# Moving the first layer-1 key tile one tile forward at each change of layer, with longer FFN steps and other banks for their products

## The chip, the cores and the metric

The kernel runs on one core of one Trainium2 chip. The metric is the device time of one execution in microseconds (us), quoted as the median of several executions. Engines are called as the profile calls them: PE is TensorE's matmuls, PEld its weight loads, DVE is VectorE, ACT is ScalarE, POOL is GpSimd, SP issues the loads.

## The reference, cut to what matters

Two identical layers of single-token decoding run one after the other, with the same weights and the same key and value cache:

```python
# B = 8 batches, one new token each, D = 640, 32 heads of Dh = 128, Sk = 4096 cached keys, Dff = 1728, bf16
x = x + attention(layernorm(x), k_cache, v_cache, wq, wo)   # layer 0
x = x + relu_ffn(layernorm(x), w1, w2)
x = x + attention(layernorm(x), k_cache, v_cache, wq, wo)   # layer 1, the same cache again
x = x + relu_ffn(layernorm(x), w1, w2)
```

Each layer reads the whole cache. Layer 1 of a batch can't begin before that batch has been through the FFN of layer 0, because its queries are made from the result.

## The kernel before

The work is cut into *visits*: one visit is one pair of heads of one batch in one layer, so 16 x 8 x 2 = 256 visits. A visit has a key tile (K) and a value tile (V). Each tile consists of four *units* of 512 KB; a unit lives in one of 26 slots of an *arena* in on-chip memory. When PE has read the last of a unit, its slot is free and the next load into it can be issued. Up to 21 slots keep tiles of layer 0 for layer 1 of the same batch, so that they need not be loaded twice.

The place that matters here is the *turn*: layer 0 of a batch ends, its FFN has to run, and then layer 1 of the batch begins. There are eight turns, one per batch. To cover the FFN, the kernel puts two layer-0 visits of the *next* batch in between ("ahead"). Call these tiles K0, V0, K1, V1, and call the first key tile of layer 1 L. L is one of the kept tiles: it needs no load, and running it sets four slots free. The order of tiles is made here, and the line with `turns` is the one in question:

```python
    slots = []
    for i in range(NV + 1):
        pair = [("K", i)] * (i < NV) + [("V", i - 1)] * (i >= 1)
        ends = i and visits[i - 1][0] == 0 and last_of[visits[i - 1][:2]] == i - 1
        turns = 0 < i < NV and visits[i][0] == 1 and visits[i - 1][0] == 0
        slots += pair[::-1] if ends or turns else pair      # before, at a turn: K0 K1 V0 V1 L
```

(The last turn differs: no next batch is left, so the two visits in between are layer-1 visits of the batch before, `turns` does not hold, and the order was K0 K1 V0 L V1 already.)

The FFN of layer 0, the norm behind it and the first two layer-1 queries form one *chain* of steps. A step is a handful of matmuls with one column each; it is put into the gap behind a unit's matmuls, so that PE always has the next unit soon. `CAP` limits how many matmuls go into one gap. The number in `own` is the matmuls of a step:

```python
CAP = 20
...
        for k in range(n_up):                        # n_up = 5: 3 of 14 row groups each
            c += [own(15, "up", k)]
            ...
        c += [own(0, "relu")] + [own(14, "down", k) for k in range(n_down)] + [own(0, "add")]   # n_down = 5
        c += [own(2, "mean"), own(0, "center")] + query(b, 0)
        c += [own(1, "var2"), own(0, "root2")] + query(b, 1)
...
        if which == "K":
            if layer:
                until(("QC", b, hp))                 # the query of this visit has to be there
```

Results of matmuls lie in three banks of the result memory (PSUM): `o_ps` (output of the V tiles), `s_ps` (scores) and `small_ps` (everything small, the FFN's products too):

```python
            h = [ffn_ps[:, :FC].rearrange("p (f b) -> p f b", b=1)] * len(up_parts)   # ffn_ps is part of small_ps
            y = ffn_ps[:, FC * B : FC * B + DC].rearrange("p (c b) -> p c b", b=1)
```

## Time and profile before

| what | value | read from |
|---|---|---|
| time | 2341.08 us, median of 3 (2338.69 to 2342.32) | the times |
| read from device memory | 988.08 MB | the page, DMA queues |
| rate between turns | 430 to 433 GB/s | the windows view |
| rate in the 40 us around a turn | 382 to 409, mean 393.8 GB/s | the windows view |
| lost per turn | 40 x (1 - 393.8/431.5) = 3.5 us, 28 us in all | worked out |

The first lines of the page are the busy time of each engine (with its share of the span and its instructions), the bytes moved, and the shares of the engines in the chain of work that ended last.

```profile
PE 1398.6 (60%) x18748; PEld 591.4 (25%) x18748; DVE 496.7 (21%) x2022; ACT 426.3 (18%) x986; POOL 59.5 (3%) x296
...
HBM read 988.08 MB, written 0.01 MB: 422 GB/s over the span
...
DMA 71%; PE 17%; ACT 6%; DVE 3%; issue 2%; SPq 0%; POOL 0%; ACTq 0%; DVEq 0%; POOLq 0%
```

No compute engine is near full, and 71% of the last chain is waiting for loads. The kernel is bound by the arrival of data, so only the places where data arrive slower than 432 GB/s can win time. The windows view of before shows these places. Its columns are the window, its length, the busy time of each engine, TensorE's clock, the DMA share and the rate in GB/s. The first three windows lie around turns, the last one between two of them. (The clock falls to 0.50 in the second half of this trace.)

```profile
190.00:230.00 40.00, 29.70 (x658) 21.35 (x658) 13.36 (x64) 6.72 (x23) 4.87 (x23) 1.00 1.00 390
475.00:515.00 40.00, 31.16 (x712) 22.96 (x710) 11.04 (x63) 5.43 (x20) 4.87 (x23) 1.00 0.99 382
1905.00:1945.00 40.00, 31.52 (x716) 23.22 (x713) 12.26 (x66) 5.81 (x20) 4.87 (x23) 0.50 1.01 402
300.00:470.00 170.00, 92.61 (x925) 29.49 (x924) 30.39 (x118) 26.56 (x55) 2.51 (x13) 1.00 1.00 431
```

At a turn the rate is about a tenth lower, and PE is at the same time about three quarters busy (31 of 40 us), against 54% (92.6 of 170) between turns. The chain of waits of before, in the turn near 1920 us, shows what PE waits for there. The columns are the start, the length in us, and what the time was spent on; L705 is the key matmul of an ahead tile, L687 the value matmul, L580 a down step.

```profile
1905.98 14.32 DMA arena<-in_A_kv_dram
...
1920.34 0.60 PE o_ps L705 x16
...
1920.96 5.74 DMA arena<-in_A_kv_dram
...
1926.74 0.60 PE o_ps L687 x4
1927.34 0.55 PE small_ps L580 x14
...
1929.23 0.58 PE o_ps L687 x4
1929.83 5.52 DMA arena<-in_A_kv_dram
...
1935.40 0.63 PE o_ps L687 x4
```

PE frees a slot and the next slot's load ends 5.5 to 5.7 us later; that load is the longest thing in the turn. With 21 slots kept, only five circulate, one slot per load; call them the *ring*. Five slots, each occupied for 5.5 us by the load and for 0.6 to 0.8 us until PE is through with it, give one slot per (5.5 + 0.7)/5 = 1.24 us, against 1.21 us at full rate.

### The profile page before, as it was taken

To read this page: it belongs to the slowest core of one execution; us is meant where nothing else is said; L and a number is where in the kernel's file an instruction comes from. 1 tells how busy PE (TensorE), PEld (TensorE's weight loads), DVE (VectorE), ACT (ScalarE), POOL (GpSimd) and SP (SyncE) were. 2 spreads that over 40 slices of the span, in tenths; PEclk is the share of its full clock that TensorE was granted. 3 is DMA by queue.
4 is the path that set the end of the run, shared out by engine and by line. 5 is a ranking of instruction groups with operands and counts; after the bars stand their busy time and mean duration, and the time that the engine had idled before them with its cause. 6 is when DMAs were issued, how large, how long until landed. Compare 5 with 4: busy or idle time off the path is not lost.

```text
span 2343.0 us, 43024 instructions
## 1 busy us (share of the span) xinstructions
PE 1398.6 (60%) x18748; PEld 591.4 (25%) x18748; DVE 496.7 (21%) x2022; ACT 426.3 (18%) x986; POOL 59.5 (3%) x296
## 2 busy tenths in 40 slices
PE   3547654576545764557545675556755567545766
PEld 1214211152111511125111241113411133111523
DVE  1113211131112211122111221112211122111312
ACT  1111211122111221112211121111211112111211
POOL 0000000000000000000000000000000000000000
PEclk9999999999999998555555555555555555555555
DMA  9999999999999999999999999999999999999997
GB/s 411 430 433 401 433 432 432 431 396 432 432 432 430 404 434 431 430 427 403 433 432 431 426 412 434 430 432 420 427 431 427 432 416 430 431 431 431 396 433 329
DMA packets 76753, 990.87 MB, mean 423 GB/s; under 512 B 8596, under 2 KB 8596, under 8 KB 36500
## 3 DMA queue, kind: packets, MB, share of 16 engines
q1 hardware_dynamic: 76564, 988.12, 99.4%
q8 instruction: 146, 2.39, 0.4%
q14 instruction: 43, 0.35, 0.0%
HBM read 988.08 MB, written 0.01 MB: 422 GB/s over the span
## 4 chain that ended last, share of the span: by engine, by line
DMA 71%; PE 17%; ACT 6%; DVE 3%; issue 2%; SPq 0%; POOL 0%; ACTq 0%; DVEq 0%; POOLq 0%
DMA arena<-in_A_kv_dram 71%; PE o_ps L687 5%; PE s_ps L695 4%; PE s_ps L705 2%; ACT P_row L755 2%; ACT o_sb L795 1%; PE small_ps L655 1%; DVE mrow L713 1%; ACT P_sb L761 1%; PE small_ps L800 1%; ACT arena L634 1%; PE small_ps L768 1%; PE small_ps L825 1%; DVE hmx L732 0%; ACT nmax L753 0%
## 5 line engine op out<-in xcount | busy, mean ns | idle before, releaser
L687 PE MATMUL o_ps<-arena,P_sb 128*4 128x512 bf16 x3952 | 584.3, 596 | 402.0 <-DMA arena<-in_A_kv_dram 401.0
L695 PE MATMUL s_ps<-arena,qz 128*4 128x512 bf16 x3040 | 410.3, 602 | 261.1 <-DMA arena<-in_A_kv_dram 249.5
L687 PEld LDWEIGHTS <-P_sb 128*4 128x4 bf16 x3952 | 107.4, 88 | 502.8 <-issue 491.7
L713 DVE TENSOR_REDUCE mrow<-s_ps 100x1 bf16<-100x512 f32 x190 | 131.8, 694 | 323.2 <-PE s_ps L695 323.2
L795 ACT CAST o_sb<-o_ps 100x512 bf16<-100x512 f32 x247 | 144.9, 587 | 289.3 <-PE o_ps L687 286.0
L753 ACT ACTIVATE nmax<-small_ps 100x1 f32<-100x1 f32 x106 | 18.1, 171 | 774.5 <-PE small_ps L742 774.5
L775 DVE CAST P_sb<-small_ps 128x64 bf16<-128x64 f32 x190 | 42.6, 224 | 523.1 <-PE small_ps L768 523.1
L695 PEld LDWEIGHTS <-qz 128*4 128x4 bf16 x3040 | 63.9, 85 | 313.7 <-issue 295.5
L705 PEld LDWEIGHTS <-arena 128*128 128x128 bf16 x4224 | 129.6, 104 | 40.8 <-DMA arena<-in_A_kv_dram 23.4
L705 PE MATMUL s_ps<-qo,arena 128*128 128x1 bf16 x3712 | 123.7, 165 | 17.2 <-ACT P_sb L761 7.6
L768 PE MATMUL small_ps<-few,P_row 100*128 100x16 bf16 x760 | 52.3, 179 | 92.1 <-ACT P_row L755 92.1
L753 ACT ACTIVATE nmax<-small_ps,q_scale 100x1 f32<-100x1 f32 x84 | 22.0, 261 | 398.7 <-PE small_ps L742 398.7
L787 DVE TENSOR_REDUCE lsum<-small_ps 128x2 f32<-128x64 f32 x240 | 53.9, 224 | 171.9 <-PE small_ps L781 171.9
L768 PEld LDWEIGHTS <-P_row 100*128 100x128 bf16 x760 | 35.0, 107 | 186.5 <-ACT P_row L755 178.2
L720 PE MATMUL small_ps<-few,mrow 100*1 100x16 bf16 x190 | 34.4, 181 | 67.6 <-DVE mrow L713 67.6
L755 ACT ACTIVATE P_row<-s_ps,nmax 100x512 bf16<-100x512 f32 x106 | 72.8, 687 | 3.4
L800 PEld LDWEIGHTS <-o_sb 100*128 100x128 bf16 x988 | 45.7, 106 | 107.2 <-ACT o_sb L795 73.8
L655 PE MATMUL small_ps<-xq,wq_sb 128*128 128x1 bf16 x1200 | 48.8, 165 | 38.9 <-DVE qo L812 33.5
L800 PE MATMUL small_ps<-few,o_sb 100*128 100x2 bf16 x988 | 65.1, 170 | 10.7 <-DVE lsum L787 2.2
L727 DVE TENSOR_REDUCE diag<-small_ps 1x2 bf16<-1x16 f32 x190 | 30.8, 162 | 186.9 <-PE small_ps L720 186.9
L720 PEld LDWEIGHTS <-mrow 100*1 100x1 bf16 x190 | 15.0, 79 | 210.8 <-DVE mrow L713 210.8
L755 ACT ACTIVATE P_row<-s_ps,nmax,q_scale 100x512 bf16<-100x512 f32 x84 | 65.3, 778 | 2.8
(225 smaller groups left out, 958.0 us busy)
## 6 DMA issues: line engine op xcount, KB each, us to landing
arena<-in_A_kv_dram SPq DMA_DIRECT2D x124, 4096.0 KB, 23.1
arena<-in_A_kv_dram SPq DMA_DIRECT2D x98, 2048.0 KB, 22.7
arena<-in_A_kv_dram SPq DMA_DIRECT2D x218, 512.0 KB, 6.5
arena<-in_A_kv_dram SPq DMA_DIRECT2D x48, 1024.0 KB, 11.3
arena<-in_A_kv_dram SPq DMA_DIRECT2D x11, 3072.0 KB, 22.4
arena<-in_A_kv_dram SPq DMA_DIRECT2D x11, 2560.0 KB, 20.5
arena<-in_A_kv_dram SPq DMA_DIRECT2D x10, 1536.0 KB, 19.7
wq_sb<-in_A_wq_dram SPq DMA_DIRECT2D x4, 1280.0 KB, 17.6
```

The source lines that it names most:

```text
L655: nc.tensor.matmul(q_ps[:, h : h + 1], lhsT=wq_sb[:, g, c, (2 * n + h) * Dh : (2 * n + h + 1) * Dh], rhs=xlns[b][:, 0, c : c + 1], start=( ...
L687: nc.tensor.matmul(o_ps[32 * c : 32 * c + CJ, :], lhsT=P_tiles[i][:, h, j : j + CJ], rhs=arena[:, at + c * CJ * Dh : at + (c + 1) * CJ * D ...
L695: nc.tensor.matmul(s_ps[32 * c : 32 * c + CJ, :], lhsT=qz[:, i % 3, c // 2, 3 - g : 3 - g + CJ], rhs=arena[:, at + c * BANK : at + (c + 1) ...
L705: nc.tensor.matmul(s_tiles[i][:, j : j + 1], lhsT=arena[:, at + n * P : at + (n + 1) * P], rhs=qo[:, b, h : h + 1], start=True, stop=True,)
L713: nc.vector.tensor_reduce(out=m_tiles[i][:OR, :1], in_=s_ps[:OR], axis=AX.X, op=ALU.max)
L720: nc.tensor.matmul(turn_ps[:1, : 4 * CJ], lhsT=m[:OR, :1], rhs=rsel[:OR], start=True, stop=True)
L755: nc.scalar.activation(out=P_rows[i][:OR], in_=s_ps[:OR], func=ACT.Exp, bias=nm[:OR, :1], scale=more)
L768: nc.tensor.matmul(P_ps[:, k * 4 * CJ : (k + 1) * 4 * CJ], lhsT=P_row[:OR, k * P : (k + 1) * P], rhs=rsel[:OR], start=True, stop=True,)
L775: nc.vector.tensor_copy(out=P_tiles[i].rearrange("p h (c k) -> p h c k", k=BANK // P), in_=P_ps.rearrange("p (k h c) -> p h c k", k=BANK / ...
L787: nc.vector.tensor_reduce(out=L, in_=(lsum2_ps if ahead[i] else lsum_ps).rearrange("p (h j) -> p h j", h=2), axis=AX.X, op=ALU.add)
L795: nc.scalar.copy(out=o_tiles[i][:OR], in_=o_ps[:OR, :].rearrange("p (j d) -> p j d", j=CJ))
L800: nc.tensor.matmul(oy[i][:, :2], lhsT=o_tiles[i][:OR, j, :], rhs=gsel[:OR, j, :], start=(j == 0), stop=(j == CJ - 1))
```

## The change

The intent: L comes one tile sooner, so that its four kept slots come free sooner and loads in larger groups can start again. The chain of FFN and queries has to end a tile sooner too, so its steps become longer, and the FFN's products are moved out of the small bank, whose reads by other engines had held up steps. (The comments behind `#` are added here.)

```diff
+UPS, DOWNS = 4, 2                      # up: 20 matmuls a step (was 15), down: 28 (was 14)
-CAP = 20
+CAP = 34
@@ the order of tiles
-        turns = 0 < i < NV and visits[i][0] == 1 and visits[i - 1][0] == 0
-        slots += pair[::-1] if ends or turns else pair
+        slots += pair[::-1] if ends else pair           # at a turn now: K0 K1 V0 L V1
@@ the chain (layer 0)
+        for f in range(0, n_f, UPS):
+            c += [own(n_c * min(UPS, n_f - f), "up", f // UPS)] + [own(0, "var"), own(0, "root")] * (f == 0)
+        c += [own(0, "relu")]
+        for k in range(0, n_c, DOWNS):
+            c += [own(n_f * min(DOWNS, n_c - k), "down", k // DOWNS)]
+        c += [own(0, "add"), (1, None), own(2, "mean"), own(0, "center")] + query(b, 0)
@@ gaps left empty, so that the small bank is read once per gap
-                chains.append(query(...))
+                chains.append([(1, None)] * 2 + query(...))
-            turned = ... else [(1, None)]
-            chains.append([...] + turned + [(1, ("L", i)), (0, ("I", i))])
+            turned = ... else [(1, None)] * (5 - ahead[i] if ahead[i] else 1)
+            chains.append([...] + turned + [(3 if ahead[i] else 1, ("L", i)), (0, ("I", i))])
@@ the banks
-    lsum2_ps = s_ps[:, 4 * NJ : 6 * NJ]
-    mean2_ps, var2_ps, q2_ps = (s_ps[:, 6 * NJ + lo : 6 * NJ + hi] for lo, hi in ((0, 1), (1, 2), (2, 4)))
+    up_ps, down_ps, mean2_ps = o_ps[:, 4 * NJ : 4 * NJ + FC], s_ps[:, 4 * NJ : 4 * NJ + DC], s_ps[:, 5 * NJ : 5 * NJ + 1]
+    lsum2_ps = s_ps[:, 5 * NJ + 8 : 7 * NJ + 8]
-            h = [ffn_ps[:, :FC].rearrange("p (f b) -> p f b", b=1)] * len(up_parts)
-            y = ffn_ps[:, FC * B : FC * B + DC].rearrange("p (c b) -> p c b", b=1)
+            h = [up_ps.rearrange("p (f b) -> p f b", b=1)] * len(up_parts)
+            y = down_ps.rearrange("p (c b) -> p c b", b=1)
... (the rest follows from these: var2 and the first query move to the small bank, the loops of the steps, the other layer's step size)
```

More of the change, by code (lines that the diff above doesn't have):

```diff
@@ L25, with plan @@
 PAD = 2048
+UPS, DOWNS = 4, 2
+LAST = 3
 AHEAD = 2
 BANK = 512
-CAP = 20
+CAP = 34
 def tile_at(NP, which, hp):
     return max(0, 2 * hp - 1) if which == "K" else min(2 * hp + 2, 2 * NP - 1)
-def plan(B, NP, n_up, n_down):
+def plan(B, NP, n_f, n_c):
     order0 = list(range(NP))
@@ L212, in finish @@
         c = []
-        for k in range(n_up):
-            c += [own(15, "up", k)]
-            if layer:
-                c += [own(0, "relu", k)]
-            elif k == min(1, n_up - 1):
-                c += [own(0, "var"), own(0, "root")]
-        if layer:
-            for k in range(n_up):
-                c += [own(15, "down", k)] + [own(0, "var"), own(0, "root")] * (k == n_up // 2)
-            return c + [own(0, "add")]
-        c += [own(0, "relu")] + [own(14, "down", k) for k in range(n_down)] + [own(0, "add")]
-        c += [own(2, "mean"), own(0, "center")] + query(b, 0)
+        if layer:
+            n = -(-n_f // LAST)
+            for k in range(n):
+                c += [own(15, "up", k), own(0, "relu", k)]
+            for k in range(n):
+                c += [own(15, "down", k)] + [own(0, "var"), own(0, "root")] * (k == n // 2)
+            return c + [own(0, "add")]
+        for f in range(0, n_f, UPS):
[4 more added lines that the diff above has]
+        c += [own(0, "add"), (1, None), own(2, "mean"), own(0, "center")] + query(b, 0)
         c += [own(1, "var2"), own(0, "root2")] + query(b, 1)
@@ L237, in plan @@
             if i + 2 < NV and visits[i + 2][0] and order1.index(visits[i + 2][2]) > 1:
-                chains.append(query(visits[i + 2][1], order1.index(visits[i + 2][2])))
+                chains.append([(1, None)] * 2 + query(visits[i + 2][1], order1.index(visits[i + 2][2])))
             pad(i)
@@ L259, in plan @@
             step()
-            turned = [(4, ("PT", i)), (0, ("PC", i))] if moving[i] else [(1, None)]
-            chains.append([(1, ("T", i)), (0, ("M2", i)), (1, ("B", i)), (0, ("E", i))] + turned + [(1, ("L", i)), (0, ("I", i))])
+            turned = [(4, ("PT", i)), (0, ("PC", i))] if moving[i] else [(1, None)] * (5 - ahead[i] if ahead[i] else 1)
+            chains.append([(1, ("T", i)), (0, ("M2", i)), (1, ("B", i)), (0, ("E", i))] + turned + [(3 if ahead[i] else 1, ("L", i)), (0, ("I", i))])
         else:
@@ L422 @@
     nc.vector.memset(o_ps, 0.0)
-    up_parts = [range(f, min(f + 3, FC)) for f in range(0, FC, 3)]
-    visits, moving, direct, ahead, ops = plan(B, NP, len(up_parts), DC)
+    visits, moving, direct, ahead, ops = plan(B, NP, FC, DC)
     s_tiles, P_rows, P_tiles, m_tiles, o_tiles, oy, invL, oT, nmax, st = ({} for _ in range(10))
@@ L536, in finish_steps @@
         b0, nb = (b, 1) if layer == 0 else (0, B)
+        n = LAST if layer else UPS
+        up_parts = [range(f, min(f + n, FC)) for f in range(0, FC, n)]
         x = xT[:, b0 : b0 + nb, :]
@@ L555, in var @@
             over_partitions(var_ps[:, :nb], st.pop("s2"))
-        def var2():
-            over_partitions(var2_ps, st.pop("s2"))
         def root():
@@ L570, in relu @@
             part = range(FC) if k is None else up_parts[k]
-            for rows, lo, hi in ((P, part[0], min(part[-1] + 1, n_full)), (Dff % P, n_full, part[-1] + 1)):
+            whole = FC if k is None else n_full
+            for rows, lo, hi in ((P, part[0], min(part[-1] + 1, whole)), (Dff % P, whole, part[-1] + 1)):
                 if rows and lo < hi:
@@ L577, in down @@
         def down(k):
-            for c, f in [(k, f) for f in range(FC)] if layer == 0 else [(c, f) for f in up_parts[k] for c in range(DC)]:
+            cs = range(k * DOWNS, min((k + 1) * DOWNS, DC))
+            for c, f in [(c, f) for c in cs for f in range(FC)] if layer == 0 else [(c, f) for f in up_parts[k] for c in range(DC)]:
                 fs = f_sizes[f]
@@ L610, in root2 @@
             r = q_scale[b] = sm.tile([P, 2], FP32, name="q_scale", bufs=2)
-            inverse_root(r[:, 0:1], var2_ps, float(Dh))
+            inverse_root(r[:, 0:1], var_ps[:, :1], float(Dh))
             nc.gpsimd.tensor_scalar(out=r[:, 1:2], in0=r[:, 0:1], scalar1=-1.0, scalar2=None, op0=ALU.mult)
-        return dict(up=up, var=var, root=root, relu=relu, down=down, add=add, mean=mean, center=center, var2=var2, root2=root2)
+        return dict(up=up, var=var, root=root, relu=relu, down=down, add=add, mean=mean, center=center, var2=var, root2=root2)
     xlns, q_scale, finishing = {}, {}, {}
@@ L650, in do_q @@
     def do_q(b, hp):
-        q_ps = st["q", b, hp] = q2_ps if hp == NP - 1 else q1_ps[:, 2 * (hp % 2) : 2 * (hp % 2) + 2]
+        q_ps = st["q", b, hp] = q1_ps[:, 2 * (hp % 2) : 2 * (hp % 2) + 2]
         g, n = divmod(hp, GP)
@@ L781, in do_l @@
         nc.tensor.matmul(
-            lsum2_ps if ahead[i] else lsum_ps, lhsT=ones_p, rhs=P_tiles[i].rearrange("p h j -> p (h j)"), start=True, stop=True
+            lsum2_ps if ahead[i] == AHEAD else lsum_ps, lhsT=ones_p, rhs=P_tiles[i].rearrange("p h j -> p (h j)"), start=True, stop=True
         )
@@ L787, in do_i @@
         nc.vector.tensor_reduce(
-            out=L, in_=(lsum2_ps if ahead[i] else lsum_ps).rearrange("p (h j) -> p h j", h=2), axis=AX.X, op=ALU.add
+            out=L, in_=(lsum2_ps if ahead[i] == AHEAD else lsum_ps).rearrange("p (h j) -> p h j", h=2), axis=AX.X, op=ALU.add
         )
```

## The prediction

> **What bounds the kernel.** Data arrival. The page has 988 MB moved at a mean 423 GB/s with DMA engines busy in every slice; in the chain that ended last, arena loads are 71%. The windows view shows 430 to 433 GB/s between the places where a layer-0 batch ends and layer 1 begins ("turns"), and 382 to 409 GB/s (mean 394) in the 40 us around each of the eight turns (near 210, 495, 785, 1075, 1355, 1645, 1925, 2200 us). That is 40 x (1 - 394/431.5) = 3.5 us lost per turn, 28 us in all: the most this change can win, 1.2%. Start and end (about 15 us each) are not touched.
>
> **Why a turn loses.** 21 of the 26 arena slots hold kept layer-1 tiles, so five circulate with one-slot loads (512 KB). In the trace such a load takes at least 5.5 us from issue to landing; with 0.6 to 0.8 us until the slot is free again, five give one slot per 1.25 us against 1.21 us at full rate. No slack: a late PE costs DMA time. (The Trainium skill, "DMA: Bandwidth & Descriptors", Anatomy of one DMA, puts a fixed 2 us on a DMA; here 5.5 less 1.2 of transfer leaves over 4.) This regime ends when the first layer-1 K tile, kept and needing no load, frees four slots. Before, that comes after 16 units (K,K,V,V): 485.4 to 505.9 in one turn. DMA drops to about 300 GB/s at 485 to 492 (queue drained by visits that load nothing) and to 320 to 370 at 500 to 505 (its echo one ring round later).
>
> **What the change does.**
> 1. Layer 1's K comes after K,K,V: 12 units, so slots come free about 5 us earlier (estimate 500.5 for 505.9), in time to fill part of the echo. The first dip stays.
> 2. The FFN and query chain must end four gaps sooner. Steps grow: up 15 to 20 matmuls, down 14 to 28 (about 30 ns each in the trace: +0.15 and +0.4 us).  I estimate PE up to 0.8 us late at the second K tile, mostly hidden, as the next V slot lands late anyway.
> 3. Products go to the output and score banks. Some waits vanish (the last up step waited 0.26 us for ACT's read of the small bank), two appear: up step 3 and down step 3 wait for DVE's 0.23 us max reduce of their bank, about 0.5 us each. (The skill, "PSUM — Partial Sum Buffer", PSUM bank collisions, says to guard by bank, not address; these waits agree.)
> 4. The last turn already ran K after the first V; there PE stood 3.3 us before that K for the query. The earlier chain should cut it below 1 us; this turn wins most, about 1.5 us.
> 5. Between turns query steps move where PE is half idle: nothing.
>
> **Sum.** 0.5 to 1 us for seven turns, 1.5 us for the last: about 6 us. Predicted 2335 us, range 2328 to 2341. Faster by over 2%: 0.5%; within 2%: 98.5%; slower by over 2%: 1%.
>
> **To be seen after.** Rate between turns unchanged; at turns about 402 in place of 394; the second dip smaller, the first alike; PE's gap before the last turn's first layer-1 K under 1 us; new short PE waits on DVE's max reduce; tail unchanged.
>
> **What would make it wrong.** Longer steps and bank waits free slots later, so turns lose as much or more; the chain misses its deadline and PE stalls before the first layer-1 K in all turns; or the loss is mostly the first dip, and nothing moves.

## More of the kernel before

The "Anatomy of one DMA" section of the Trainium skill's page "DMA: Bandwidth & Descriptors" puts a fixed cost of about 2.0 us on one DMA beside the bytes. That figure is for loads issued by GpSimd; here SP issues them.

## The result, and the profile after

| | median us | lowest to highest | runs |
|---|---|---|---|
| before | 2341.42 | 2338.69 to 2342.42 | 6 |
| after | 2348.64 | 2347.98 to 2349.80 | 6 |

The ratio of the two is 1.0033 (95% interval 1.002 to 1.0046): after is about 7 us slower. Ratios in this text are the mean time of one kernel's fast runs over that of the other's of the same rounds, so they are not quite the ratios of the medians quoted. The difference is within 2%, as nearly all of the predicted chance had it, but the predicted time of 2335 us and its range up to 2341 us were wrong, and so was the sign.

The page of after shows the same work and the same bytes:

```profile
PE 1391.8 (59%) x18748; PEld 578.7 (25%) x18748; DVE 496.7 (21%) x2014; ACT 425.6 (18%) x986; POOL 59.0 (3%) x296
...
HBM read 988.08 MB, written 0.01 MB: 421 GB/s over the span
...
DMA 73%; PE 17%; ACT 5%; DVE 3%; issue 2%; SPq 0%; ACTq 0%; DVEq 0%; POOL 0%; POOLq 0%
```

Nothing was added or removed; the shares of the whole span hide what happened. The windows view of after, with the windows shifted to where its turns lie, is the first useful view:

```profile
190.00:230.00 40.00, 31.69 (x731) 22.46 (x727) 14.21 (x67) 6.84 (x24) 4.83 (x23) 1.00 0.98 374
476.00:516.00 40.00, 33.61 (x804) 24.44 (x803) 11.73 (x66) 6.84 (x24) 4.83 (x23) 1.00 0.99 391
1908.00:1948.00 40.00, 32.30 (x733) 22.78 (x730) 12.43 (x65) 6.66 (x23) 4.83 (x23) 0.50 0.98 381
300.00:470.00 170.00, 89.29 (x894) 28.63 (x893) 29.66 (x114) 25.95 (x54) 2.49 (x13) 1.00 1.00 431
```

The rate between turns is unchanged at 431 GB/s. Over all eight turns the mean is 388.1 GB/s (374 to 396), where before had 393.8 and the prediction had 402. So a turn of after loses 40 x (1 - 388.1/431.5) = 4.02 us against 3.50 us, and eight turns lose 4.2 us more. That is just the difference of the two traces' spans, 2347.2 and 2343.0 us: the loss is in the turns and nowhere else. The traces of all 17 kernels of this text say the same: their spans run from 2337.7 to 2350.7 us, but the span less the loss in its eight turns (counted as in the table below, to 45 us) is 2312.1 to 2313.7 us in every one. (The traced execution of before took 2344.78 us, some 3 us more than its median. One trace is one sample, and a few us of the 7 can't be found by comparing just two.)

The chain of waits of after, again in the turn near 1920 us, shows a different picture from before's. L707 is now the key matmul, L552 an up step, L582 a down step, L717 the max reduce of a visit's scores, L590 the addition of the FFN's result, L741 the step that spreads the maximum, L763 ACT's exponential, L493 the mean, L689 the value matmul.

```profile
1900.34 20.62 DMA arena<-in_A_kv_dram
...
1921.01 0.58 PE o_ps L707 x16
1921.59 0.53 PE o_ps L552 x20
...
1926.81 1.01 PE s_ps L582 x28
...
1927.94 0.39 PE s_ps L707 x11
1928.32 0.91 issue
1929.23 0.27 PE s_ps L707 x5
...
1929.50 1.02 PE s_ps L582 x28
...
1931.07 0.24 DVE mrow L717
1931.35 0.61 PE s_ps L582 x14
1932.07 0.23 DVE xT L590
...
1933.30 0.17 PE small_ps L741
...
1933.70 0.47 ACT P_sb L763 x2
...
1934.22 0.20 PE s_ps L493 x2
...
1934.95 0.53 PE o_ps L689 x4
```

In before, loads of 5.5 us stood in this chain; PE waited for data. In after, there is no load in it from 1921.0 us until after L has begun at 1936.34: data wait for PE. PE first works back to back, alternating units with long steps, then hands small results to and fro with DVE and ACT. It took 16.58 us from the first unit of K0 to the first of L, which is 12 units, or 1.38 us per unit, where the loads could have delivered one per 1.21 us. Before, the same stretch held 16 units in 19.49 us, or 1.22 us per unit.

The lateness of PE can be read unit by unit: it is the time from the landing of a unit's load to PE's first weight load on it. (A value matmul loads its weights from the scores and not from the slot, so at V tiles this can be a little less than the true lateness. In the first turn every kernel is 1.6 us late at K0 already; it is left out where kernels are compared below.) In before's turn near 1920 us it is at most 0.35 us. In the same turn of after it is 0.7 us at the third unit of K1, 1.5 us at the fourth, 1.7 us at the first unit of V0 and 2.3 us at the third. In all eight turns of after the fourth unit of K1 is 0.4 to 1.7 us late and the third unit of V0 0.9 to 2.3 us.

Late units mean slots freed late. The following table was worked out from the two traces and, since the traced run of before was a long one, from a third trace of before with harmless work added (experiment e10, 2340.49 us in its traced run). It gives the loss in us against 433 GB/s, counted from 5 us before a turn's first unit of K0, mean of the first seven turns:

| from the first unit of K0 to | 10 us | 20 us | 30 us | 45 us |
|---|---|---|---|---|
| before | 1.66 | 2.52 | 3.37 | 3.64 |
| before, other trace (e10) | 1.52 | 2.30 | 2.84 | 3.08 |
| after | 1.43 | 3.59 | 4.08 | 4.32 |

Up to 10 us the three are alike: the first dip is there in all, as predicted. Between 10 and 20 us after loses 2.16 us where the others lose 0.8. In this stretch its rate falls to 314 GB/s (12.5 to 15 us), about one round of the five slots (6 us) behind the late units. From 20 to 30 us it recovers soon (0.49 us lost), sooner than this trace of before (0.85 us) and about as soon as the other (0.54 us). Whatever the earlier L wins there, it is smaller than what was lost ahead of it.

Waits that begin in the result banks are seen in the timeline of after, the same turn. In brackets is the idle time of the engine just before, and what ended it.

```profile
1924.42 0.67 PE L552 MATMUL o_ps<-xf,w_sb 128*128 128x1 bf16 x20 [0.32 <-DVE mrow L717]
...
1929.23 0.27 PE L707 MATMUL s_ps<-qo,arena 128*128 128x1 bf16 x5 [0.91 <-issue]
...
1931.35 0.60 PE L582 MATMUL s_ps<-hT,w_sb 128*128 128x1 bf16 x14 [0.32 <-DVE mrow L717]
...
1934.22 0.19 PE L493 MATMUL s_ps<-s1h,few 128*128 128x1 bf16 x2 [0.76 <-ACT P_sb L763]
```

The third up step waits for DVE's max reduce on the output bank, and the last down step for the one on the score bank. These were predicted. The last line was not: the mean of the norm now lies in the score bank in the same gap in which ACT's exponential reads the scores, and stands behind it. The line with "issue" is a stop without a semaphore; it is taken up at e12. The Trainium skill's page "PSUM — Partial Sum Buffer", section "PSUM bank collisions raise a hardware error", says to guard results by bank and quadrant and not by address. This trace agrees: the steps wait for reads of other columns of their bank, at 0.32 and 0.76 us each.

### The profile page after: what moved, and what is told of

The parts are those of the page before. It is cut to its first block, busy times and chain, and to the rows that moved or that the text cites. A ratio compares the mean times of both kernels' runs of the same rounds, so it can differ in the third digit from the quotient of the medians.

```text
span 2347.2 us, 43033 instructions
## 1 busy us (share of the span) xinstructions
PE 1391.8 (59%) x18748; PEld 578.7 (25%) x18748; DVE 496.7 (21%) x2014; ACT 425.6 (18%) x986; POOL 59.0 (3%) x296
## 3 DMA queue, kind: packets, MB, share of 16 engines
q8 instruction: 146, 2.39, 0.4%
## 4 chain that ended last, share of the span: by engine, by line
DMA 73%; PE 17%; ACT 5%; DVE 3%; issue 2%; SPq 0%; ACTq 0%; DVEq 0%; POOL 0%; POOLq 0%
DMA arena<-in_A_kv_dram 73%; PE o_ps L689 5%; PE s_ps L697 4%; PE s_ps L707 3%; ACT P_row L757 1%; ACT o_sb L797 1%; ACT arena L636 1%; PE small_ps L657 1%; ACT P_sb L763 1%; PE s_ps L582 1%; PE small_ps L802 1%; PE small_ps L827 1%; DVE mrow L715 1%; PE small_ps L770 1%; PE o_ps L552 1%
## 5 line engine op out<-in xcount | busy, mean ns | idle before, releaser
L689 PE MATMUL o_ps<-arena,P_sb 128*4 128x512 bf16 x3952 | 575.2, 597 | 465.6 <-DMA arena<-in_A_kv_dram 465.5
L697 PE MATMUL s_ps<-arena,qz 128*4 128x512 bf16 x3040 | 420.0, 598 | 244.4 <-DMA arena<-in_A_kv_dram 232.3
L689 PEld LDWEIGHTS <-P_sb 128*4 128x4 bf16 x3952 | 104.8, 85 | 582.4 <-issue 574.0
L707 PEld LDWEIGHTS <-arena 128*128 128x128 bf16 x4224 | 131.9, 104 | 25.3 <-DMA arena<-in_A_kv_dram 19.9
L707 PE MATMUL s_ps<-qo,arena 128*128 128x1 bf16 x3712 | 128.7, 165 | 6.3 <-DMA arena<-in_A_kv_dram 4.5
L657 PEld LDWEIGHTS <-wq_sb 128*128 128x128 bf16 x1280 | 45.9, 105 | 68.7 <-issue 68.7
L783 PE MATMUL small_ps<-P_sb,few 128*128 128x64 bf16 x248 | 56.5, 228 | 9.8 <-DVE P_sb L777 6.3
## 6 DMA issues: line engine op xcount, KB each, us to landing
arena<-in_A_kv_dram SPq DMA_DIRECT2D x10, 2560.0 KB, 20.7
```

Of the source, the lines that this page charges most:

```text
L657: nc.tensor.matmul(q_ps[:, h : h + 1], lhsT=wq_sb[:, g, c, (2 * n + h) * Dh : (2 * n + h + 1) * Dh], rhs=xlns[b][:, 0, c : c + 1], start=( ...
L689: nc.tensor.matmul(o_ps[32 * c : 32 * c + CJ, :], lhsT=P_tiles[i][:, h, j : j + CJ], rhs=arena[:, at + c * CJ * Dh : at + (c + 1) * CJ * D ...
L697: nc.tensor.matmul(s_ps[32 * c : 32 * c + CJ, :], lhsT=qz[:, i % 3, c // 2, 3 - g : 3 - g + CJ], rhs=arena[:, at + c * BANK : at + (c + 1) ...
L707: nc.tensor.matmul(s_tiles[i][:, j : j + 1], lhsT=arena[:, at + n * P : at + (n + 1) * P], rhs=qo[:, b, h : h + 1], start=True, stop=True,)
L783: nc.tensor.matmul(lsum2_ps if ahead[i] == AHEAD else lsum_ps, lhsT=ones_p, rhs=P_tiles[i].rearrange("p h j -> p (h j)"), start=True, stop ...
```

## The experiments

Three theories were tried. The first: longer steps and waits on banks make PE late in the second K tile and the first V tile, slots come free late, and the loads pay. The second, its rival: the new place of L is what costs. As first put (e1, e2) this meant that all FFN and query work has to fit 12 units; later (e11 to e15) it meant that the place costs by itself, whatever PE does. The two meanings have to be kept apart below. The third: PE's instruction fetch stops it in the denser bursts (the "issue" gap above). An overview first; differences are of the medians to before of the same chip job:

| kernel | median us | to before | ratio (95%) |
|---|---|---|---|
| e1 after, old place of L | 2348.74 | +7.3 | 1.0033 (1.002 to 1.0046) |
| e2 before, new place of L only | 2348.46 | +7.1 | 1.0028 (1.0014 to 1.0042) |
| e3 after, short steps | 2352.37 | +11.0 | 1.0048 (1.0036 to 1.0061) |
| e4 after, mean ahead of the exponential | 2348.10 | +6.7 | 1.0027 (1.0014 to 1.0039) |
| e5 before, long steps only | 2352.45 | +10.0 | 1.0044 (1.003 to 1.0057) |
| e6 before, banks only | 2346.79 | +4.4 | 1.0019 (1.0006 to 1.0031) |
| e7 before, empty gaps only | 2343.92 | +1.5 | 1.0009 (0.9996 to 1.0021) |
| e8 long steps and new place | 2348.36 | +5.9 | 1.0026 (1.0014 to 1.0039) |
| e9 before, delay in the ring | 2344.93 | +3.6 | 1.0015 (1.0001 to 1.0029) |
| e10 before, delay elsewhere | 2340.64 | -0.7 | 0.9998 (0.9985 to 1.001) |
| e11 up steps of 20 and new place | 2349.39 | +8.1 | 1.0032 (1.0019 to 1.0044) |
| e12 after, instruction blocks shifted | 2348.85 | +7.5 | 1.0029 (1.0016 to 1.0042) |
| e13 new place, first query not waited for | 2339.53 | -1.9 | 0.9993 (0.998 to 1.0005) |
| e14 chain spread, new place | 2348.32 | +6.9 | 1.0029 (1.0016 to 1.0041) |
| e15 chain spread, old place | 2343.14 | +1.7 | 1.0008 (0.9995 to 1.0022) |

### e1 and e2: the place and the rest, each alone

After with the old order of tiles, and before with the new one:

```diff
@@ e1, in after
-        slots += pair[::-1] if ends else pair
+        turns = 0 < i < NV and visits[i][0] == 1 and visits[i - 1][0] == 0
+        slots += pair[::-1] if ends or turns else pair
@@ e2, in before
-        turns = 0 < i < NV and visits[i][0] == 1 and visits[i - 1][0] == 0
-        slots += pair[::-1] if ends or turns else pair
+        slots += pair[::-1] if ends else pair
```

> The changed kernel with the old place of layer 1's first K tile (K,K,V,V, then K); long FFN steps, new banks and paddings stay. Theory 1 (the longer steps and bank waits make PE late in the second K tile and the first V tile, and late frees starve the five-slot ring): PE is still 0.7 to 1.7 us late there and the time stays at 2346 to 2350 us. Rival, theory 2 (the new place is what costs, as all FFN and query work must fit 12 units): PE's lateness is worked off over the second V tile and the time returns to 2340 to 2343 us.

> The kernel before with only the new place of layer 1's first K tile; short FFN steps in the small bank. Theory 1: PE stays on time (under 0.4 us late) up to the last unit of the first V tile and then stops about 3 us for the query, as the last turn of before already does; 12 units take about 17 us in all turns, time 2343 to 2348 us. Theory 2: the same stop, and the whole slowdown or more, 2347 us or above. If the place alone helps as predicted, under 2340 us.

Each alone cost 7 us, and the two together, which is after, cost 7 us too. e1 came out in the range of the first theory; e2, at 2348.46 us, just above the first theory's range and inside the rival's. The effects don't add, so neither part can be called the cause by its size. But e1 shows that the slowdown doesn't need the new place, and e2 that it doesn't need the long steps or the new banks. The traces differ. In e1 PE is late by 0.9 to 2.4 us at V0, as in after; from 20 to 30 us behind K0 it loses 0.92 us where after loses 0.49, so the earlier L does fill part of a hole, once lateness has made one. In e2 the short steps keep PE within 0.5 us of the loads, but then the chain isn't ready when L is due. The timeline of e2, turn near 1059 us, shows the last down step (L579), the last unit of V0 (L686), the mean (L491), the query (L654) and the first matmuls of L (L704):

```profile
1072.18 0.62 PE L579 MATMUL small_ps<-hT,w_sb 128*128 128x1 bf16 x14
...
1074.40 0.60 PE L686 MATMUL o_ps<-arena,P_sb 128*4 128x512 bf16 x4 [1.60 <-DMA arena<-in_A_kv_dram]
...
1075.49 0.19 PE L491 MATMUL s_ps<-s1h,few 128*128 128x1 bf16 x2 [0.32 <-DVE lsum L786]
...
1076.14 0.41 PE L654 MATMUL s_ps<-xq,wq_sb 128*128 128x1 bf16 x10 [0.46 <-DVE xq L605]
...
1076.80 0.56 PE L704 MATMUL s_ps<-qo,arena 128*128 128x1 bf16 x16 [0.25 <-ACT qo L662]
```

Behind the last V0 unit at 1074.40 hardly anything but the chain's serial end is left, and L begins 2.4 us after it. The 12 units took 16.0 to 17.3 us in e2's turns. So there are two ways to lose at a turn: PE late at units whose load is there (e1), or L late because the query isn't ready (e2). The trace of after shows the first: in all its turns L begins 0.6 us after the last V0 unit, which is back to back.

### e3 and e4: after with short steps, and with the mean ahead

```diff
@@ e3, in after
-UPS, DOWNS = 4, 2
+UPS, DOWNS = 3, 1
-CAP = 34
+CAP = 20
@@ e4, in after: the mean counts as one matmul and goes ahead of the step that starts the exponential
-        ... (1, None), own(2, "mean"), ...
+        ... (1, None), own(1, "mean"), ...
-            turned = ... [(1, None)] * (5 - ahead[i] if ahead[i] else 1)
+            turned = ... [(1, None)] * (4 if ahead[i] else 1)
```

> The changed kernel with the old step lengths (up 15, down 14 matmuls, cap 20); new place and new banks stay. Theory 1: PE lateness at the second K tile falls from 0.6 to 1.7 us to under 0.5 us, the chain ends later and PE stops about 3 us before layer 1's first K; net 2342 to 2347 us. Theory 2: no better than the changed kernel, 2347 to 2351 us. Theory 3 (PE waits for its own instruction blocks, which the denser bursts of one-column matmuls use up faster than 16 KB fetches arrive): the unexplained gaps of 0.6 to 1.1 us inside a run of matmuls, seen in five turns of the changed kernel, are gone.

> The changed kernel, but the two matmuls of the mean are issued before (not behind) the steps that let ACT read the score bank, and the sum of the first visit's weights comes one gap later. In the changed kernel the mean waits for ACT's exp on the same bank, so that PE stands about 2.5 us between the second and third unit of the first V tile. Theory 1: the third unit of that V tile is late by under 0.7 us in place of 0.9 to 2.3 us, and 0.5 to 1 us per turn comes back: 2341 to 2345 us. Theory 2 or 3: that gap shrinks, but other lateness keeps the time within 2 us of the changed kernel's.

Short steps in after's banks cost more (+11.0 us, above every range that had been set): the up step waits 0.83 us for the exponential on the output bank, PE is late by 1.0 to 1.6 us at the third unit of V0 (2.2 us in the last turn), and the chain ends late as in e2. With after's banks and place, long steps are therefore a help (+7.2 against +11.0 us); with the old banks they make no difference in the new place (e8 and e2), and in the old place they are a harm (e5). In e4 the trace shows the wait gone: the mean has no bracket any more, and the next unit waits for its load again.

```profile
1071.12 0.22 PE L493 MATMUL s_ps<-s1h,few 128*128 128x1 bf16 x2
...
1071.81 0.60 PE L689 MATMUL o_ps<-arena,P_sb 128*4 128x512 bf16 x4 [0.31 <-DMA arena<-in_A_kv_dram]
```

In this trace the third unit of V0 is at most 0.6 us late, as the first theory had asked for, and L begins 14.7 to 15.9 us after K0, no later than in e13 below. But the median fell by only 0.5 us against after (2348.10 and 2348.64), less than the spread of the runs, so the range of the first theory was missed and that of the others met. (The traced run, 2344.88 us, was the fastest of the five.) The unforeseen wait is real, and is not what the 7 us hang on; nor is it enough that the whole chain fits. PE is still 0.4 to 1.4 us late at the fourth unit of K1.

### e5 to e8: the parts alone in before

e5 is before with `UPS, DOWNS = 4, 2` and `CAP = 34` alone; e6 has the moved banks alone; e7 has the empty gaps alone; e8 is e5 with the new order.

```diff
@@ e5, in before
+UPS, DOWNS = 4, 2
-CAP = 20
+CAP = 34
... (and the step loops of the change)
@@ e6, in before
-    lsum2_ps = s_ps[:, 4 * NJ : 6 * NJ]
+    up_ps, down_ps, mean2_ps = o_ps[:, 4 * NJ : ...], s_ps[:, 4 * NJ : ...], s_ps[:, 5 * NJ : ...]
... (and the other lines on banks of the change)
@@ e7, in before
-        c += [own(2, "mean"), ...
+        c += [(1, None), own(2, "mean"), ...
-                chains.append(query(...))
+                chains.append([(1, None)] * 2 + query(...))
... (and the later L of the ahead visits)
@@ e8 is e5 with
+        slots += pair[::-1] if ends else pair
```

> The kernel before with only the longer FFN steps (up 20, down 28 matmuls, cap 34), products still in the small bank, old place of layer 1's K. Theory 1 in two parts: if the length of the steps makes PE late, its lateness at the second K tile is 0.5 us or more and the time 2344 to 2349 us; if it is the waits on the new banks, PE is under 0.5 us late and the time stays at 2339 to 2343 us.

> The kernel before with only the new banks (up products in the output bank, down products in the score bank); old steps, old place. If the bank waits are the cause: PE waits for DVE's max reduce at the third up step (0.3 us) and for ACT's exp at the last up step and in the first V tile, is 0.8 us or more late there, and the time is 2345 to 2351 us. If not, 2339 to 2343 us.

> The kernel before with only the later places of the query steps and of the weight sums (one read of the small bank per gap). No theory sees a cost here: 2339 to 2343 us. Above 2345 us it would be a cause that neither theory has.

> The kernel before with the longer steps and the new place of layer 1's first K, but the old banks: the query is ready before that K, so the 3 us stop of the run with the place alone should go. If the bank waits are the cause of the slowdown: PE under 0.5 us late, no stop, 2336 to 2342 us, and this is the version that gains. If the place itself or the length of the steps costs: 2345 us or more.

Long steps alone cost most, 10.0 us, more than the first theory's range. In e5 PE is 1.2 to 1.7 us late at the fourth unit of K1 and up to 2.2 us at V0 (2.6 us in the last turn). Its timeline shows both a longer step and waits that a longer step brings about, since it pushes steps of the visit into gaps where another engine reads their bank:

```profile
1069.64 1.15 PE L582 MATMUL small_ps<-hT,w_sb 128*128 128x1 bf16 x28
...
1073.47 0.24 PE L783 MATMUL s_ps<-P_sb,few 128*128 128x64 bf16 x1 [0.32 <-DVE mrow L717]
...
1076.71 0.41 PE L657 MATMUL s_ps<-xq,wq_sb 128*128 128x1 bf16 x10 [0.76 <-ACT P_sb L763]
```

The banks alone cost 4.4 us, with PE late by up to 0.9 us at V0 (1.3 us in the last turn) and at V1 up to 1.3. The empty gaps cost 1.5 us, which the interval does not tell from nothing. In sum the parts alone would be +10.0 + 4.4 + 1.5 + 7.1 = 23 us; together they are +7.2. Parts that make the same units late don't add. Note the sign of the new place: with short steps it costs 7.1 us (e2 against before), with long steps it wins 4.1 us (2352.45 in e5, 2348.36 in e8), and in after it is worth nothing (e1). What the place is worth depends on what else PE is late with.

### e9 and e10: is lateness at a turn what costs, and how much?

32 pairs of weight load and one-column matmul, on data that are there, were put into before: in e9 after the third unit of K1 in each turn, in e10 eight visits sooner, where the loads are far ahead.

```diff
+            if op[0] == "mm" and op[1] == "K" and op[3] == 2 and any(op[2] == t + 1 for t in first_ahead):   # e10: t - 8
+                for _ in range(32):
+                    nc.tensor.matmul(row_ps[:, P - 1 : P], lhsT=ident, rhs=onesb_c, start=True, stop=True)
```

> The kernel before plus 32 useless one-column matmuls (about 1.1 us of PE) once per turn, behind the third unit of the second K tile ahead, where only five slots circulate; 256 matmuls in all, results unused. Theory 1 (in that stretch a late PE is a late load and lost DMA time): PE is about 1 us late for a few units and the time rises by 4 to 9 us, to 2346 to 2351 us. If lateness of that size is hidden (so that something else costs the changed kernel its time): under 2344 us.

> The same 32 matmuls once per turn, but eight visits before the turn, where loads are queued tens of us ahead. Theory 1: no change, 2340 to 2344 us, which with the run before shows that it is the place of the delay and not the work. If PE's own work mattered: as much slower as the run before.

Both kernels issue the same loads in the same order as before. In e9 the fourth unit of K1 was 0.9 to 1.0 us late, and the lateness wore off over the next one to six units. That cost 3.6 us, or 0.45 us per turn, just below the range of the first theory; by the interval it is 0.2 to 6.8 us, so 0.03 to 0.85 us per turn. The same work outside the turns cost nothing that could be measured (e10). This tells what kind of time is lost: a microsecond of PE costs nothing measurable where units are loaded far ahead, and something like half of it where five slots circulate. A delay of 1 us that starts at one unit gives half of the 7 us; after's PE stays late for six units, up to 2.3 us.

### e11: only the up steps longer

```diff
@@ before with the new order, and
+UPS, DOWNS = 4, 1        # up 20, down 14, CAP 20, banks as before
```

> The kernel before with the new place of layer 1's K, up steps of 20, but down steps of 14 and the old banks: PE should be late by 0.5 to 0.8 us at the second K tile in place of 0.9 to 1.9 us, and the chain ends with one gap to go, so that PE stops under 1.5 us before layer 1's K. If lateness and stop together set the time, 2342 to 2346 us, between before and the changed kernel; if the place costs by itself, 2347 us or more.

This was meant to be a better version: a shorter chain without the steps of 28. PE was late by about 0.5 us at most (0.8 us in the seventh turn), but L began 2.0 us after the last V0 unit, 0.9 us of it with PE idle. The time was 2349.39 us, no better than after and in the range that had been set for the rival. Trading lateness for a stop moves the cost and does not remove it.

### e12: instruction fetch

The page lists a queue of 146 packets and 2.39 MB for instructions, so 16 KB each. In after PE is idle for 0.47 to 0.91 us without a semaphore in five of its turns, like the one at 1928.32 us above. Counting the weight loads of the trace from its first, they come at counts of 92 to 95 beyond a multiple of 128, so bound to blocks of 128. (The expectations measure from weight load to weight load and count from another start: 0.6 to 1.1 us, 99 to 102.) Before has none in its turns, its other trace (e10) two of 0.57 us. The Trainium skill's page "Runtime: NRT & Kernel Launch", section "Instruction fetch mechanics", says that instructions come in blocks of 16 KiB (256 instructions) and that the cost of a block boundary is "mostly hidden". A block of 256 is 128 pairs of weight load and matmul, and the gaps lie one block apart. In e12, 64 pairs were put before the first operation of after, which moves the boundaries by half a block:

```diff
+        for _ in range(64):
+            nc.tensor.matmul(P_ps[:, :1], lhsT=ident, rhs=onesb_c, start=True, stop=True)
```

> The changed kernel with 64 useless matmul pairs (half a 16 KB instruction block) at the very start, where PE waits for data. Theory 3 (the unexplained PE gaps of 0.6 to 1.1 us are waits for instruction blocks): any such gap again comes at the same count of weight loads modulo 128 (99 to 102), which is now another place of the schedule, half a block away, and just after a 16 KB fetch has landed; the time changes by under 3 us, 2345 to 2351 us. If the gaps belong to the schedule, they stay at the same operations and their count modulo 128 moves by 64.

The gaps moved with the blocks: they stand at other places of the program, before matmuls at 494.38 us (0.43 us of idle PE) and 1644.34 us (1.19 us), again at counts of 95 and 93. So they belong to the blocks and not to the program. That they are waits for the fetch fits this, but no view shows the wait itself. The time stayed (2348.85 against 2348.64 us), with two such gaps of 1.6 us together in this trace where after's had five of 3.2 us. This speaks against a large share, but these are one trace each, and the run doesn't price the gaps. The trace of e9 has such gaps too, in three turns (0.79 to 1.18 us), and e9 is 3.6 us slower than before, not 7; a part of e9's 3.6 us may be theirs. In e3 and e6 no turn has such a gap of 0.4 us or more, and they cost 11.0 and 4.4 us. So the gaps don't make the 7 us alone, and time is lost without them; what share they have in them is left open.

### e13: the new place without the query's deadline

If the place itself were at fault, it should cost also when the chain has no deadline. e13 is e2 with one thing more: L doesn't wait for the query of its own visit, but uses a stale one that has long been there. The result of these visits is wrong; its 529 loads and the order of its tiles are those of e2, one by one. (The comparison with the reference passed all the same, so a pass proves little here.)

```diff
@@ e2, and
             if layer:
-                until(("QC", b, hp))
+                if hp != order1[0]:
+                    until(("QC", b, hp))
-            h = 2 * hp + c // 2
+            h = c // 2 if layer and hp == NP - 1 else 2 * hp + c // 2
```

> The kernel before with only the new place of layer 1's first K, whose scores are taken with another head's query so that it waits for nothing (a wrong result on purpose; the work is the same). Theory 1 (only late or stopping PE costs): no stop, PE under 0.5 us late, and the time is 2337 to 2342 us, no more than before. Theory 2 (the place costs by itself): 2346 us or more.

The median is 2339.53 us, 1.9 us below before (the interval of the ratio includes 1; it runs from 4.7 us faster to 1.2 us slower) and 8.9 us below e2, whose base is the same within 0.03 us. The three turns that were read in the windows view have 384, 395 and 408 GB/s, mean 396, where the same three of before have 390, 382 and 395, mean 389. The chain of waits, turn near 1057 us, has loads in it again:

```profile
1046.97 13.90 DMA arena<-in_A_kv_dram
...
1060.91 0.60 PE o_ps L705 x16
...
1061.53 6.03 DMA arena<-in_A_kv_dram
...
1067.60 0.60 PE o_ps L687 x4
...
1072.79 0.56 PE s_ps L705 x16
```

PE is late by 0.5 us at most, and L (the last line) begins 14.8 to 16.0 us after K0. It comes 1.5 us after the last V0 unit, where e2 has 2.4 us: PE still stands for 0.56 us, for the mean and for DVE's read of the score bank, but no longer for the query. With the same loads in the same order, the place is innocent: what costs in e2 is that L has to wait for its query. But the place isn't worth anything that could be seen either: the loss of the first seven turns, whose order changed, is 21.8 us in all in e13, 21.6 us in the better trace of before (e10) and 25.5 us in the other. The last turn, whose order is the same in both, lost 2.87 us against 4.2 in e10, since its L no longer waits for the query; that alone is most of the 1.9 us.

### e14 and e15: the chain spread out

A last try to keep the new place with a real query: up steps of 20, down steps of 14, 14, 14 and 28, each put first in its gap; in the new place (e14) and the old one (e15).

```diff
+UPS = 4
+DOWN_GROUPS = [[0], [1], [2], [3, 4]]
-CAP = 20
+CAP = 34
... (and the step loops)
-        for c in sorted(now, key=lambda c: len(c) > 1 and not c[1][0]):
+        for c in sorted(now, key=lambda c: (not c[0][1] or c[0][1][0] != "C", len(c) > 1 and not c[1][0])):
@@ e14 only
+        slots += pair[::-1] if ends else pair
```

> A correct version: new place, old banks, up steps of 20, down steps of 14, 14, 14 and 28 (the long one beside a V unit, where PE has little to do), FFN steps first in each gap so that they don't queue behind reads of the small bank. Theory 1: PE late by 0.5 us or less up to layer 1's K and no stop: 2337 to 2343 us. Theory 2: 2346 us or more.

> The same steps in the old place. Theory 1: 2338 to 2344 us, at most 3 us from the run before, by what the place gives when PE is on time. Theory 2: faster than the run before by 4 us or more.

In the new place this was 2348.32 us, like after and e2. In the old place, with less lateness of PE at the third unit of V0 (0.4 us on average, 0.8 in e14), it was 2343.14, which the interval doesn't tell from before. The pair differs by 5.2 us, and only by the order: with a chain of this length, four units less of cover cost about 5 us. By the ranges set beforehand, both runs came out on the side of the rival. They do not show that the place costs by itself, though: what the first theory asked for, PE on time and no stop, was not reached (in e14 PE is 0.9 to 1.6 us late at the second unit of V0, and L comes 1.6 us after its last unit), and e13, where the query's deadline was gone, did not lose. No kernel with a correct result was measurably faster than before.

## Why the prediction was right or wrong

- **What bounds the kernel, and where it can win** (right). The rate between turns did not change (431), and the whole difference of the two traces lies in the turns.
- **Point 1, L sooner frees slots sooner, "in time to fill part of the echo"** (the slots do come sooner, but the gain isn't there). L began 15.6 to 16.6 us after K0 instead of 19.4 to 20.7, so 3 to 5 us sooner. Where PE had made a hole, this filled part of it (0.49 us lost from 20 to 30 us in after, 0.92 in e1). Where it had not, there was little to fill: in e13, with the place alone and no deadline, the seven turns lost as much as in before's better trace (21.8 and 21.6 us), where 0.5 to 1 us per turn had been put. The echo that the prediction read at 500 to 505 us was one turn of a trace that was itself 3 us longer than the median; in the other trace of before the stretch from 20 to 30 us costs 0.54 us, so there was hardly 1 us per turn to be won there.
- **Point 2, "The FFN and query chain must end four gaps sooner ... I estimate PE up to 0.8 us late at the second K tile, mostly hidden"** (this is the step that failed). The steps themselves were costed well: a down step of 28 took 1.01 us in the chain against 0.55 for 14, +0.46 where +0.4 was put. What failed is how late PE gets, and above all "mostly hidden". PE was 0.4 to 1.7 us late at the fourth unit of K1, up to about twice the estimate; it did not catch up there but was 0.9 to 2.3 us late at V0. And it was not hidden: the DMA hole between 10 and 20 us costs 2.16 us per turn instead of 0.8. This needs no new place: e1, with the same steps and banks and 16 units of cover, is as late and as slow. In before, the steps alone cost 10.0 us (e5) and the banks alone 4.4 us (e6), and e9 shows that a delay of 1 us is not hidden there but costs about 0.45 us ("no slack" was too strong in turn). The same sentence, "must end four gaps sooner", hides a second loss: with short steps PE is on time, but the chain misses its deadline. 12 units then take 16.0 to 17.3 us (e2), where without the wait for the query they take 14.8 to 16.0 us (e13), and 7 us are lost in that way too. In after's trace L doesn't wait, so it is the first loss that one sees there.
- **Point 3, waits on banks** (right, and incomplete). Both foreseen waits are there at 0.32 us of idle PE. The mean behind ACT's exponential on the score bank was not foreseen. It was 0.76 us of idle PE, but its removal (e4) won only 0.5 us of the median. The banks as a whole, alone in before, cost 4.4 us (e6).
- **Point 4, the last turn** (right in kind, too large in size). The 3.3 us had been misread: they run from the weight load of the last V0 unit to that of L (2195.96 to 2199.28 us), and for 1.3 us of them PE waits for that unit's own data. From the unit's first matmul to L's it was 2.4 us; in after it is 0.6 us, which is back to back, so the stop went as predicted. The loss of the turn fell from about 4.75 to 4.35 us, so by 0.4 us and not 1.5. In e13, where this L waits for no query, the same turn lost 2.87 us: the size was there, but not with the real chain.
- **Point 5, nothing between turns** (right).
- **What would make it wrong** named two outcomes, longer steps and bank waits freeing slots later, and the chain missing its deadline. Both came: the first in after and e5, the second in e2 and e11. They were given too little weight in the range. For the second, the length of the whole chain against 12 units was never added up, although every duration for it was in before's trace; before's last turn, with 12 units in 17.02 us and L 2.4 us after the last V0 unit, was the example in plain sight. The prediction read it as something that the change mends, not as what the new order would do to the seven others.

What stays open: the split of after's 7 us between long steps, bank waits and fetch gaps. The parts don't add (23 us alone, 7 together), and a kernel with long steps but no added waits was not made. Versions as different as e2, e4, e8, e11 and e14 all end at 2348 to 2349 us. One would like to say that one chain is too long for 12 units by the same amount whichever way it is laid out, but e1 ends there too, with 16 units, and so does e4, whose 12 units took no longer than those of e13. Why so many versions end at the same time is not shown.

## What to carry to other kernels

When work that hides behind loads gets fewer loads to hide behind, add up the whole chain, with its serial end, and compare it with the loads' time: here 16.0 to 17.3 us (e2) against 14.8 to 16.0 (e13). That it fits is not enough: where a few buffers circulate with little slack, lateness of the consumer at single units isn't fully absorbed but comes back about one round of the buffers later (e1, e9). Price a reordering first by a run that has the new order but not its deadline (as e13): it shows in one go about what the order can win at most, here 2 us of 2341, or 4.7 at the end of the interval.

## What the Trainium skill lacked or had wrong

- "DMA: Bandwidth & Descriptors", "Anatomy of one DMA": a fixed cost of about 2.0 us, for loads issued by GpSimd. Here, with SP issuing and the DMA engines loaded, a 512 KB load took 5.4, 6.1 and 7.6 us from issue to landing (medians) with three, four and five other units under way, a good part of it probably time behind their bytes. That neither confirms nor contradicts the 2.0 us. The section has no figure for a loaded queue, and for a ring of few buffers that is the one that counts.
- "Runtime: NRT & Kernel Launch", "Instruction fetch mechanics": the block of 16 KiB agrees with the page's 146 packets (2.39 MB), and "mostly hidden" holds for before's turns. In dense bursts of one-column matmuls with loaded DMA engines PE stood idle for 0.43 to 1.19 us at block-bound places (after and e12), so "mostly hidden" is not always so, if these stops are the fetch's.
- "PSUM — Partial Sum Buffer", "PSUM bank collisions raise a hardware error": agrees, and lacks a price. Moving small products to a bank that other engines read in the same gap cost 0.32 to 0.76 us of idle PE per wait, and 4.4 us in all when done alone (e6).
- No page that was consulted says what lateness of a consumer costs when few buffers circulate: about 1 us of PE put in once per turn cost 0.45 us a turn (e9; interval 0.03 to 0.85), the same work where loads are far ahead nothing measurable (e10).
